# First block of a fused scan and expert kernel: the second product in plain fp32, and the weight remainders moved

## The chip, the cores and the metric

The kernel runs on one core of one Trainium2 chip. The core has TensorE (PE, matrix products, with its weight loads shown apart as PEld), VectorE (DVE), ScalarE (ACT), GpSimd (POOL) and SyncE (SP, which here only issues DMAs). The metric is the device time of one execution in microseconds. Three executions of the kernel before took 844.75, 845.05 and 848.32 us; their median is 845.05 us.

## What is computed

```python
# 1. a gated linear scan: q, k, v, alpha are [4, 8, 768, 48]
for t in range(S):
    state = alpha[:, :, t, :, None] * state + einsum('bhd,bhe->bhde', k[:, :, t], v[:, :, t])
    y[:, :, t] = einsum('bhd,bhde->bhe', q[:, :, t], state)
x = y.transpose(0, 2, 1, 3).reshape(3072, 384)
# 2. a dense layer: w_in [384, 2048], w_out [2048, 384]
h = x @ w_in
x = (h - np.tanh(h)) @ w_out
# 3. a top-1 mixture of 8 experts on these rows: argmax of x @ w_gate picks the expert,
#    out[mask] = gate_w * sigmoid(x @ w_output_gate) * (relu(x @ w1[e]) @ w2[e])
```

Everything is wanted in float32. The router takes an argmax of products, so part 2 has to be close to full float32 precision.

## The kernel before

**Tiling.** The 3072 tokens are eight blocks `j` of 384 (`TB`). In a block the dense layer runs over 16 slices `f` of 128 hidden features (`NF`). A slice is one `h_step` (the first product: three chunks of 128 input features, then tanh on ScalarE and h - tanh(h) on VectorE) and one `x_step` (the second product, for three groups of 128 tokens, added up over the 16 slices in three PSUM banks `x0` to `x2`). The scan is cut into units `u` of a block and a pair of heads, four units to a block; the units of block `j + 1` run between the dense slices of block `j`, one unit to four slices. The four slices `f % 4` of such a group are called phases 0 to 3 here: phase 0 has `score` and `update` of the unit, phase 2 its `readout`, phase 3 `turn_k`, the scan over its decays (`prep_q1`) and `scale_k`.

**Split products.** A product of two float32 matrices is made of three products in `F32R`: each operand is split into a rounded copy (`WH`, `gg[:, 0]`) and a remainder (`WL`, `gg[:, 1]`), and high x high, low x high and high x low are added up. So an `h_step` is nine matmuls of 384 columns (L401) and an `x_step` nine of 400 columns (L425). The 400 are 384 of `w_out` and 16 that stand for the two router matrices: `gate_turn` transposes a slice of `w_out` through PSUM (L369, copied by ScalarE at L371), and `gate` multiplies it by the router's weights (L377).

**Weights.** They arrive as 64-bit words that hold float64 values. `narrow` turns them into float32 on VectorE with three integer operations (L332, L334, L336), here on 768 columns at a time: 384 of `w_in` and 384 of `w_out`. `split_w` then writes the rounded copy on ScalarE (L361) and the remainder on GpSimd (L362). All of this is done in the first block, in `first_block`, for slices that lie one or two ahead of the products; two slices are prepared ahead of the block. From the second block on the weights only are read.

**Order.** In the first block the instructions of each engine stand in the order in which the program is written: `first_block(f)` writes the split of slice `f + 1`, the conversion of slice `f + 2`, the first product of slice `f`, then `head` (the `gate` of the slice and the unit's matmuls), h - tanh(h), `middle` (the second product of slice `f - 1` and the unit's vector work), and last `gate_turn(f + 1)`. From the second block on a scheduler sets the order. An engine takes its instructions strictly in order.

Of the kernel before, what the change touches and what calls it, by code (L numbers as in the profile page):

```python
# [63 lines left out]
def tile_kernel(ctx, tc, aps, outs):  # L64
# [12 lines left out]
    wp = wst_.enter_context(tc.tile_pool(name="wp", bufs=1))  # L77
    moe = ExitStack()
# [36 lines left out]
    WH = wp.tile([128, NF, DM + DG], F32R, name="WH")  # L115
    WL = wp.tile([128, NF, DM + DG], F32R, name="WL")
# [222 lines left out]
    def load_w(f):  # L339
        if wide:  # L340
            t = stg.tile([128, 2 * DM], I64, tag="wst", name="wst")
        else:
            t = stg3.tile([128, 2 * DM], F32, tag="w32", name="w32")
        wt[f] = t
        sp.dma_start(out=t, in_=aps["wio"][f].rearrange("p s c -> p (s c)"))

    px, gw, gated = {}, {}, {}

    def conv(f):
        w = wt.pop(f)  # L350
        if wide:
            t = stg3.tile([128, 2 * DM], I32, tag="w32", name="w32")
            yield from narrow(t, w)
            w = t.bitcast(F32)
        gw[f] = w
        if f + STG < NF:
            load_w(f + STG)

    def split_w(f):
        c = slice(0, 2 * DM)  # L360
        act.copy(WH[:, f, c], gw[f])  # L361
        pool.tensor_tensor(out=WL[:, f, c], in0=gw[f], in1=WH[:, f, c].bitcast(F32), op=ALU.subtract)  # L362


    def gate_turn(f):
        ps = psa.tile([128, 512], F32, tag="at", name="pso")
        w = gw.pop(f)
        for k in range(KC):
            pe.transpose(ps[:, k * 128:(k + 1) * 128], w[:, DM + k * 128:DM + (k + 1) * 128], ident)  # L369
# [4 lines left out]
    def gate(f):  # L374
# [20 lines left out]
    def h_begin(j, f, kcs):  # L395
        if kcs[0] == 0:
            begun[f] = psh.tile([128, 512], F32, tag="h", name="psh")
        for kc in kcs:
            c = slice(kc * 128, (kc + 1) * 128)
            for n, (w, x) in enumerate(((WH, 0), (WH, 1), (WL, 0))):  # L400
                pe.matmul(begun[f][:, 0:TB], w[:, f, c], xT[j][:, x, kc], start=(kc + n == 0), stop=(kc == KC - 1 and n == 2))  # L401

    def h_step(j, f, between=()):
# [4 lines left out]
        for step in between[:1]:  # L408
# [5 lines left out]
        for step in between[1:]:  # L414
            step()
# [3 lines left out]
    def x_step(j, f, gg):  # L419
        if f == 0:  # L420
            px[j] = [psx.tile([128, 512], F32, tag=f"x{a}", name=f"x{a}") for a in range(NA)]
        for a in range(NA):
            n = 0
# [279 lines left out]
    for u in range(NP):  # L703
        weave(chain(u))
        if u + 1 < NP:
# [10 lines left out]
            for f in list(gw):  # L716
                split_w(f)
# [474 lines left out]
```

## Time and profile before

| | |
|---|---|
| median of three executions | 845.05 us |
| the profiled execution | 845.42 us |
| its span | 843.6 us |
| PE busy, matmuls | 806.4 us (96%) |
| DVE busy | 478.1 us (57%) |
| ACT busy | 350.5 us (42%) |
| POOL busy | 164.0 us (19%) |
| mean granted TensorE clock | 0.974 of full |

The page also cuts the span into 40 slices of 21 us. Each digit below is a tenth: the busy share of an engine, or, in the row PEclk, the granted clock of TensorE. The first block of the dense layer lies in the slices 3 to 7.

```
PE   6788889999999999999999999999999999999995
DVE  6878886856756765765765654455443434434321
POOL 1023242011200110010020020012222414424321
PEclk 8798899999999999999999999999999999999998
```

Such a page is read from the stage outward: the totals say that PE is nearly always busy, but they are a mean over stages, and in the first slices PE has gaps, its clock is lower, and VectorE is as busy as PE.

### The profile page before, as it was taken

The numbers are of one execution on the slowest core, as the hardware profiler recorded it, in microseconds if no ns is written. First come the engines' busy times: TensorE is split into PE (matmuls) and PEld (weight loads), VectorE is DVE, ScalarE is ACT, GpSimd is POOL, SyncE is SP. The second block draws the span as 40 slices with busy tenths as digits, with TensorE's granted clock in tenths as the row PEclk, the third lists the DMA queues.
The fourth block names the chain that finished last, engine by engine and source line by source line (L and its number), as shares of the span: only waits on it lengthen the run. The fifth ranks groups of instructions, "written<-read, shape, count | busy, mean of one in ns | idle before, by whom it ended". The sixth has DMA issues, their size and how long they took to land.

```text
span 843.6 us, 17092 instructions
## 1 busy us (share of the span) xinstructions
PE 806.4 (96%) x6736; PEld 761.5 (90%) x6736; DVE 478.1 (57%) x1002; ACT 350.5 (42%) x783; POOL 164.0 (19%) x136
## 2 busy tenths in 40 slices
PE   6788889999999999999999999999999999999995
PEld 4577889999999999999999999999999999999995
DVE  6878886856756765765765654455443434434321
ACT  4544454533433433443433433335343434445431
POOL 1023242011200110010020020012222414424321
PEclk8798899999999999999999999999999999999998
DMA  9465442773322332242232220024335336325400
GB/s 272 144 223 184 144 125 57 236 244 100 102 83 64 83 103 64 68 124 65 65 103 82 64 76 19 15 99 135 133 136 202 115 105 217 103 102 206 155 26 30
DMA packets 64361, 98.55 MB, mean 117 GB/s; under 512 B 20236, under 2 KB 52769, under 8 KB 64273
## 3 DMA queue, kind: packets, MB, share of 16 engines
q1 hardware_dynamic: 60864, 87.91, 33.9%
q0 software_dynamic: 3408, 9.47, 3.0%
q8 instruction: 55, 0.90, 0.4%
q14 instruction: 34, 0.27, 0.1%
HBM read 72.13 MB, written 16.25 MB: 105 GB/s over the span
## 4 chain that ended last, share of the span: by engine, by line
PE 80%; DVE 6%; issue 5%; DMA 3%; ACT 2%; SPq 1%; POOL 1%; POOLq 0%; DVEq 0%; ACTq 0%
PE x L425 24%; PE psh L401 22%; PE o L950 11%; PE psf L922 10%; PE psy L302 4%; PE psy L238 3%; PE psu L264 2%; DVE w L334 2%; DMA raw<-raw 2%; PE pst L222 1%; PE pst L901 1%; ACT kt L200 1%; PE pso L377 1%; DMA s<-w 1%; DVE w L336 1%
## 5 line engine op out<-in xcount | busy, mean ns | idle before, releaser
L425 PE MATMUL x<-WH,gg 128*128 128x400 f32 x768 | 215.4, 356 | 1.0 <-DVE gg L416 0.7
L401 PE MATMUL psh<-xT,WH 128*128 128x384 f32 x768 | 204.2, 343 | 1.3 <-DMA xT<-y 1.2
L425 PEld LDWEIGHTS x<-WH,gg 128*128 128x128 f32 x768 | 140.5, 191 | 6.2 <-DVE gg L416 1.7
L401 PEld LDWEIGHTS psh<-xT,WH 128*128 128x128 f32 x768 | 138.4, 189 | 3.1 <-issue 1.6
L425 PE MATMUL x<-WL,gg 128*128 128x400 f32 x384 | 133.5, 349 | 0.0
L401 PE MATMUL psh<-xT,WL 128*128 128x384 f32 x384 | 130.1, 339 | 0.0
L411 DVE TENSOR_TENSOR t<-psh,t 128x384 f32<-128x384 f32 x128 | 70.9, 554 | 98.9 <-ACT t L407 98.2
L407 ACT ACTIVATE t<-psh 128x384 f32<-128x384 f32 x128 | 62.6, 489 | 130.1 <-PE psh L401 129.1
L950 PE MATMUL o<-hi,hh 128*128 128x384 f32 (+2 forms) x440 | 115.1, 338 | 0.0
L922 PE MATMUL psf<-xe,hi 128*128 128x256 f32 (+6 forms) x432 | 109.4, 338 | 0.0
L416 DVE TENSOR_TENSOR gg<-t,gg 128x384 fp32r<-128x384 f32 x128 | 73.7, 575 | 52.6 <-ACT gg L413 51.9
L413 ACT CAST gg<-t 128x384 fp32r<-128x384 f32 x128 | 65.5, 511 | 73.3 <-DVE t L411 72.3
L928 DVE SCALAR_TENSOR_TENSOR hh<-psf,hh 128x384 fp32r<-128x384 f32 (+3 forms) x96 | 40.9, 447 | 91.1 <-ACT hh L926 91.0
L950 PEld LDWEIGHTS o<-hi,hh 128*128 128x128 f32 (+2 forms) x440 | 78.3, 185 | 1.2 <-DVE hh L928 0.2
L922 PEld LDWEIGHTS psf<-xe,hi 128*128 128x128 f32 x432 | 75.8, 188 | 2.7 <-issue 0.3
L950 PE MATMUL o<-lo,hh 128*128 128x384 f32 (+1 forms) x232 | 77.7, 337 | 0.0
L926 ACT ACTIVATE hh<-psf 128x256 fp32r<-128x256 f32 (+6 forms) x72 | 34.8, 484 | 94.1 <-PE psf L922 78.6
L197 POOL TENSOR_TENSOR kt<-kh,rP 128x384 f32<-128x384 f32 x24 | 20.3, 845 | 273.0 <-PE psy L239 230.8
L425 PEld LDWEIGHTS x<-WL,gg 128*128 128x128 f32 x384 | 73.1, 190 | 0.1
L401 PEld LDWEIGHTS psh<-xT,WL 128*128 128x128 f32 x384 | 72.4, 189 | 0.6
L922 PE MATMUL psf<-xe,lo 128*128 128x256 f32 (+6 forms) x216 | 72.0, 333 | 0.0
L857 POOL TENSOR_TENSOR lo<-s,hi 128x768 fp32r<-128x768 f32 (+1 forms) x24 | 48.9, 2039 | 94.8 <-ACT hi L856 94.3
(141 smaller groups left out, 1130.0 us busy)
## 6 DMA issues: line engine op xcount, KB each, us to landing
raw<-raw SPq DMA_DIRECT2D x32, 579.5 KB, 4.5
wst<-wio SPq DMA_DIRECT2D x16, 768.0 KB, 4.4
s<-w SPq DMA_DIRECT2D x24, 512.0 KB, 3.8
s<-w SPq DMA_DIRECT2D x32, 384.0 KB, 5.3
xT<-y SPq DMA_DIRECT2D x96, 72.0 KB, 2.3
rows<-blank SPq DMA_DIRECT2D x8, 772.0 KB, 4.9
WV<-vw SPq DMA_DIRECT2D x32, 144.0 KB, 2.3
VZ<-vn SPq DMA_DIRECT2D x60, 72.0 KB, 2.4
```

Of the source, the lines that this page charges most:

```text
L302: pe.matmul(o, w, m, start=(c + x == 0), stop=(x == 1), skip_group_check=True)
L401: pe.matmul(begun[f][:, 0:TB], w[:, f, c], xT[j][:, x, kc], start=(kc + n == 0), stop=(kc == KC - 1 and n == 2))
L407: act.activation(out=t, in_=ps[:, 0:TB], func=AF.Tanh)
L411: dve.tensor_tensor(out=g, in0=ps[:, 0:TB], in1=t, op=ALU.subtract)
L413: act.copy(gg[:, 0], g)
L416: dve.tensor_tensor(out=gg[:, 1], in0=g, in1=gg[:, 0].bitcast(F32), op=ALU.subtract)
L425: pe.matmul(px[j][a][:, 0:DG], gg[:, gi, a * 128:(a + 1) * 128], w[:, f, DM:], start=(f == 0 and n == 0), stop=(f == NF - 1 and n == 2))
L857: (dve, pool)[i % 2].tensor_tensor(out=lo, in0=t, in1=hi.bitcast(F32), op=ALU.subtract)
L922: pe.matmul(ps[:, 0:n], w[:, kc, fs], xe[:, x, kc], start=(i == 0), stop=(i == 3 * KC - 1))
L926: act.activation(out=hh[:, 0:n], in_=ps[:, 0:n], func=AF.Relu)
L928: dve.scalar_tensor_tensor(out=hh[:, o:o + c.stop - c.start], in0=ps[:, c], scalar=0.0, in1=hh[:, c].bitcast(F32), op0=ALU.max, op1=ALU.su ...
L950: pe.matmul(po[q][m][0:p.stop - p.start, 0:DM], hh[:, p], w[:, f], start=(f == 0 and i == 0), stop=(f == NFE - 1 and i == len(parts) - 1))
```

## The change

In the first block the second product is one plain fp32 matmul of the unsplit `h - tanh(h)` with the unsplit weights `WR` (three instructions of 400 columns to a slice in place of nine; the profile shows a plain fp32 matmul as two). The split of the activations (L413, L416) falls away in this block. The weights have separate tiles now: `IH`, `IL` for `w_in`, `OH`, `OL` and the unsplit `WR` for `w_out`. `narrow` runs on 384 columns twice, in place of 768 once, and writes the half for `w_out` into `WR`. The remainders of `w_in` (`low_in`) are made on VectorE, not on GpSimd. Those of `w_out` (`low_out`) are made on VectorE too, but only two of them at the end of the first block and the other 14 in the second block, which is the first that reads them; their tiles take over the places of `WR`. GpSimd does no weight work any more. `scale_k` is written after `gate_turn(f + 1)` in phase 3, so that ScalarE copies `wT` first. The lines that choose between 64-bit and 32-bit weights, and the allocation of the tiles, are left out of the diff.

```diff
     def conv(f):
-        w = wt.pop(f)
         if wide:
-            t = stg3.tile([128, 2 * DM], I32, tag="w32", name="w32")
-            yield from narrow(t, w)
-            w = t.bitcast(F32)
-        gw[f] = w
+            t = stg3.tile([128, DM], I32, tag="w32", name="w32")
+            plain(f)
+            w = wt.pop(f)
+            yield from narrow(t, w[:, 0:DM])
+            gw[f] = t.bitcast(F32)
+            act.copy(IH[:, f], gw[f])
+            yield from narrow(WR[f][:, 0:DM].bitcast(I32), w[:, DM:])
...
-    def split_w(f):
-        c = slice(0, 2 * DM)
-        act.copy(WH[:, f, c], gw[f])
-        pool.tensor_tensor(out=WL[:, f, c], in0=gw[f], in1=WH[:, f, c].bitcast(F32), op=ALU.subtract)
+    def low_in(f):
+        dve.tensor_tensor(out=IL[:, f], in0=gw.pop(f), in1=IH[:, f].bitcast(F32), op=ALU.subtract)
+
+    def low_out(f):
+
+        OL[f] = wo.tile([128, DG], F32R, tag="w", name="OL")
+        dve.tensor_tensor(out=OL[f], in0=WR.pop(f), in1=OH[:, f].bitcast(F32), op=ALU.subtract)
...
-        c = slice(2 * DM, 2 * DM + 2 * E)
-        gl = ap2.tile([128, 2 * E], F32, tag="gl", name="gl")
-        act.copy(gl, pl)
-        act.copy(WH[:, f, c], pl)
-        gated[f] = gl, c
-
-    def gate_low(f):
-        gl, c = gated.pop(f)
-        dve.tensor_tensor(out=WL[:, f, c], in0=gl, in1=WH[:, f, c].bitcast(F32), op=ALU.subtract)
+        act.copy(WR[f][:, DM:DG], pl)
...
         g = t
         dve.tensor_tensor(out=g, in0=ps[:, 0:TB], in1=t, op=ALU.subtract)
+        if j == 0:
+            return g
         gg = g3.tile([128, 2, TB], F32R, tag="gg", name="gg")
         act.copy(gg[:, 0], g)
...
-            for gi, w in ((0, WH), (1, WH), (0, WL)):
-                pe.matmul(px[j][a][:, 0:DG], gg[:, gi, a * 128:(a + 1) * 128], w[:, f, DM:],
...
+            ts = slice(a * 128, (a + 1) * 128)
+            parts = ((gg[:, ts], WR[f]),) if j == 0 else ((gg[:, 0, ts], OH[:, f]), (gg[:, 1, ts], OH[:, f]), (gg[:, 0, ts], OL[f]))
+            for n, (g, w) in enumerate(parts):
+                pe.matmul(px[j][a][:, 0:DG], g, w, start=(f == 0 and n == 0), stop=(f == NF - 1 and n == len(parts) - 1))
...
             for f in list(gw):
-                split_w(f)
+                low_in(f)
...
-        if f + 1 < NF:
-            split_w(f + 1)
-        if nconv < NF:
-            weave(conv_next())
+        new = [conv_next()] if nconv < NF else []
...
             elif ph == 2:
                 readout(u)
+            act.copy(OH[:, f], WR[f])
+            if f + 1 < NF:
+                low_in(f + 1)
+            for g in new:
+                for _ in range(4 if wide else 0):
+                    next(g)
 
         def middle():
+            weave(*new)
...
                 x_step(*pend)
                 turn_k(u)
                 weave(prep_q1(u))
-                scale_k(u)
                 weave(prep_q2(u))
...
-        gg = h_step(0, f, (head, middle))
-        gate_low(f)
+        gg = h_step(0, f, (head,))
+        middle()
+        if f >= NF - 2:
+            low_out(f - NF + 2)
...
         if f + 1 < NF:
             gate_turn(f + 1)
-        else:
+        if ph == 3:
+            scale_k(u)
+        if f == NF - 1:
...
+            if j == 1 and f + 2 < NF:
+                low_out(f + 2)
             gg = h_step(j, f)
```

**VectorE, a slice of phase 3 in the first block, before.** `w` is the float32 word being built, `t` becomes h - tanh(h), `P`, `rP` and `X` are the decays of the unit.

```order
L332 TENSOR_SCALAR w_817<-wst 128x768
L334 SCALAR_TENSOR_TENSOR w_817<-wst,w_817 128x768
L336 SCALAR_TENSOR_TENSOR w_817<-wst,w_817 128x768
L411 TENSOR_TENSOR t<-psh,t 128x384
L184 SCALAR_TENSOR_TENSOR P<-raw,ones_116 128x391
L187 TENSOR_SCALAR rP<-P 128x6
L188 RECIPROCAL rP<-rP 128x6
L204 TENSOR_TENSOR X_120<-raw,P 128x384
```

The same place now:

```order
L374 TENSOR_TENSOR IL<-w_785,IH 128x384
L336 TENSOR_SCALAR w_831<-wst 128x384
L338 SCALAR_TENSOR_TENSOR w_831<-wst,w_831 128x384
L340 SCALAR_TENSOR_TENSOR w_831<-wst,w_831 128x384
L336 TENSOR_SCALAR WR<-wst 128x384
L419 TENSOR_TENSOR t<-psh,t 128x384
L338 SCALAR_TENSOR_TENSOR WR<-wst,WR 128x384
L340 SCALAR_TENSOR_TENSOR WR<-wst,WR 128x384
L188 SCALAR_TENSOR_TENSOR P<-raw,ones_119 128x391
L191 TENSOR_SCALAR rP<-P 128x6
L192 RECIPROCAL rP<-rP 128x6
L208 TENSOR_TENSOR X_124<-raw,P 128x384
```

The remainder `IL` stands ahead, the conversion is two chains of three short operations, and four of the six stand ahead of h - tanh(h), as all three did before.

**ScalarE, from phase 3 into phase 0, before.** `kt` are the six pieces of `scale_k`, `wT` is the transposed slice for the next `gate`.

```order
L381 CAST WH<-pso 128x16
L413 CAST gg<-t 128x384
L224 COPY ktok<-pst 128x384
L200 ACTIVATE kt<-kh,rP 128x64 x6
L371 COPY wT<-pso 128x384
L361 CAST WH<-w_817 128x768
L407 ACTIVATE t<-psh 128x384
```

The same place now:

```order
L780 CAST OH<-WR 128x400
L366 CAST IH<-w_831 128x384
L228 COPY ktok<-pst 128x384
L387 COPY wT<-pso 128x384
L204 ACTIVATE kt<-kh,rP 128x64 x6
L415 ACTIVATE t<-psh 128x384
L394 COPY WR<-pso 128x16
```

`wT` has moved ahead of the six pieces of `kt`, and the 768-column rounding of the next slice's weights has become two copies (`OH`, `IH`) further ahead.

**VectorE, where the first block ends and the second begins, before** (from the last slice's split of the activations on; `r` and `lz` are the rows handed to the router).

```order
L416 TENSOR_TENSOR gg<-t,gg 128x384
L386 TENSOR_TENSOR WL<-gl,WH 128x16
L176 TENSOR_TENSOR kh<-raw,Ex 128x384
L184 SCALAR_TENSOR_TENSOR P<-raw,ones_116 128x391
L187 TENSOR_SCALAR rP<-P 128x6
L204 TENSOR_TENSOR X_120<-raw,P 128x384
L188 RECIPROCAL rP<-rP 128x6
L411 TENSOR_TENSOR t<-psh,t 128x384
```

The same place now, from the decays of the last slice's unit to h - tanh(h) of the second block's first slice:

```order
L192 RECIPROCAL rP<-rP 128x6
L208 TENSOR_TENSOR X_123<-raw,P 128x384
L379 TENSOR_TENSOR OL<-WR,OH 128x400 x3
L180 TENSOR_TENSOR kh<-raw,Ex 128x384
L379 TENSOR_TENSOR OL<-WR,OH 128x400
L188 SCALAR_TENSOR_TENSOR P<-raw,ones_119 128x391
L379 TENSOR_TENSOR OL<-WR,OH 128x400
L191 TENSOR_SCALAR rP<-P 128x6
L208 TENSOR_TENSOR X_124<-raw,P 128x384
L419 TENSOR_TENSOR t<-psh,t 128x384
```

The five remainders `OL` in this piece stand between the decays of the coming units. One stands ahead of the piece, and ten follow, the last of them ahead of h - tanh(h) of the second block's fifth slice. From the middle of the second block on, the rows of every engine are the same as before but for names and numbers.

## Rows read from the trace of the kernel before

**Rows 1.** ScalarE's timeline, first block: start us, us, engine, line, operation, tiles; slices 0, 4, 8, 12, 15

```profile
46.06 0.49 ACT L407 ACTIVATE t<-psh 128x384 f32<-128x384 f32 x1 [2.17 <-PE psh L401]
...
71.16 0.48 ACT L407 ACTIVATE t<-psh 128x384 f32<-128x384 f32 x1
...
97.09 0.48 ACT L407 ACTIVATE t<-psh 128x384 f32<-128x384 f32 x1
...
123.76 0.48 ACT L407 ACTIVATE t<-psh 128x384 f32<-128x384 f32 x1
...
142.05 0.49 ACT L407 ACTIVATE t<-psh 128x384 f32<-128x384 f32 x1 [1.03 <-PE psh L401]
```

**Rows 2.** Busy us of PE, PEld, DVE, ACT, POOL, then clock, in two stretches

```profile
71.00:97.00 26.00, 22.77 (x197) 21.80 (x197) 21.83 (x35) 13.26 (x38) 8.13 (x4) 0.89 0.52 168
147.00:200.00 53.00, 52.84 (x527) 49.54 (x527) 36.24 (x88) 23.87 (x58) 6.46 (x10) 1.00 0.67 210
```

**Rows 3.** Timelines of VectorE and GpSimd, slice 7 (phase 3)

```profile
88.67 0.55 DVE L332 TENSOR_SCALAR w<-wst 128x768 int32<-128x768 int32 x1
89.26 2.48 DVE L334 SCALAR_TENSOR_TENSOR w<-wst,w 128x768 int32<-128x768 int32 x1
91.78 0.96 DVE L336 SCALAR_TENSOR_TENSOR w<-wst,w 128x768 int32<-128x768 int32 x1
...
88.80 2.12 POOL L362 TENSOR_TENSOR WL<-w,WH 128x768 fp32r<-128x768 f32 x1 [4.01 <-DVE y L311]
```

**Rows 4.** TensorE's timeline and the chain of waits (start us, us), slice 8 (phase 0)

```profile
96.50 1.46 PE L377 MATMUL pso<-wg,wT 128*128 128x16 f32 x6 [3.23 <-ACT wT L371]
...
99.44 1.16 PE psu L264 x12
100.60 3.02 PE x L425 x9
```

**Rows 5.** TensorE's timeline, slice 14 (phase 2)

```profile
134.41 0.49 PE L369 MATMUL pso<-cst,w 128*128 128x128 f32 x3
134.66 0.60 PE L401 MATMUL psh<-xT,WH 128*128 128x384 f32 x2
...
136.33 0.73 PE L377 MATMUL pso<-wg,wT 128*128 128x16 f32 x6
137.00 0.47 PE L302 MATMUL psy<-X,SS 48*64 48x64 f32 x8
...
138.22 0.63 PE L425 MATMUL x<-WH,gg 128*128 128x400 f32 x2
...
139.96 0.49 PE L369 MATMUL pso<-cst,w 128*128 128x128 f32 x3
```

**Rows 6.** TensorE's timeline, slice 0 (score, update)

```profile
46.52 0.27 PE L238 MATMUL psy<-X,kt 48*64 48x64 f32 x1
...
47.37 0.72 PE L264 MATMUL psu<-VZ,ktok 128*64 128x96 f32 x12
```

**Rows 7.** Lines L238, L264, L222 and L401 alone: count: ns min/median/max

```profile
L238 PE MATMUL psy<-X,kt x336: 218/218/366, 46.5 to 526.0; 48*64 48x64 f32 x168
...
L264 PE MATMUL psu<-VZ,ktok x360: 246/246/421, 9.3 to 526.7; 128*64 128x96 f32 x180
...
L222 PE MATMUL pst<-cst,kh x96: 270/272/475, 7.3 to 521.2; 128*128 128x128 f32 x96
...
L401 PEld LDWEIGHTS psh<-xT,WH x768: 186/188/333, 39.5 to 587.7; 128*128 128x128 f32 x192
```

**Rows 8.** Timelines ahead of the first block: VectorE, ScalarE, TensorE

```profile
29.48 0.55 DVE L244 TENSOR_TENSOR X<-pss,cst 128x384 f32<-128x384 f32 x1
...
29.82 0.83 ACT L361 CAST WH<-w 128x768 fp32r<-128x768 f32 x1
...
45.26 0.58 PE L401 MATMUL psh<-xT,WH 128*128 128x384 f32 x2 [1.22 <-DMA xT<-y]
```

**Rows 9.** Line L416 alone, VectorE, 384 columns, two inputs

```profile
L416 DVE TENSOR_TENSOR gg<-t,gg x128: 528/559/2182, 49.0 to 590.2; 128x384 fp32r<-128x384 f32 x128
```

More of the change, by code (lines that the diff above doesn't have):

```diff
@@ L112, in tile_kernel @@
     ones1 = ap1.tile([128, AW], F32, name="ones1")
-    WH = wp.tile([128, NF, DM + DG], F32R, name="WH")
-    WL = wp.tile([128, NF, DM + DG], F32R, name="WL")
+    IH = wp.tile([128, NF, DM], F32R, name="IH")
+    IL = wp.tile([128, NF, DM], F32R, name="IL")
+    OH = wp.tile([128, NF, DG], F32R, name="OH")
+    OL, WR = {}, {}
     X0 = [ap1.tile([128, TB], F32, name=f"X0{i}") for i in range(2)]
@@ L340, in load_w, with plain @@
         if wide:
[L341 to L345 removed]
+            wt[f] = t = stg.tile([128, 2 * DM], I64, tag="wst", name="wst")
+            sp.dma_start(out=t, in_=aps["wio"][f].rearrange("p s c -> p (s c)"))
+        else:
+            gw[f] = stg3.tile([128, DM], F32, tag="w32", name="w32")
+            plain(f)
+            sp.dma_start(out=gw[f], in_=aps["wio"][f, :, 0])
+            sp.dma_start(out=WR[f][:, 0:DM], in_=aps["wio"][f, :, 1])
     px, gw, gated = {}, {}, {}
+    def plain(f):
+        WR[f] = (ap1 if f == NF - 1 else wo).tile([128, DG], F32, tag="w", name="WR")
     def conv(f):
[L350 removed]
         if wide:
[L352 to L355 removed]
+            t = stg3.tile([128, DM], I32, tag="w32", name="w32")
+            plain(f)
+            w = wt.pop(f)
[3 more added lines that the diff above has]
+            yield from narrow(WR[f][:, 0:DM].bitcast(I32), w[:, DM:])
+        else:
+            act.copy(IH[:, f], gw[f])
         if f + STG < NF:
             load_w(f + STG)
[L359 to L362 removed]
+    def low_in(f):
[3 more added lines that the diff above has]
+        dve.tensor_tensor(out=OL[f], in0=WR.pop(f), in1=OH[:, f].bitcast(F32), op=ALU.subtract)
     def gate_turn(f):
         ps = psa.tile([128, 512], F32, tag="at", name="pso")
[L367 removed]
         for k in range(KC):
[L369 removed]
+            pe.transpose(ps[:, k * 128:(k + 1) * 128], WR[f][:, k * 128:(k + 1) * 128], ident)
         wT = g3.tile([128, KC, 128], F32, tag="gg", name="wT")
@@ L399, in h_begin @@
             c = slice(kc * 128, (kc + 1) * 128)
-            for n, (w, x) in enumerate(((WH, 0), (WH, 1), (WL, 0))):
+            for n, (w, x) in enumerate(((IH, 0), (IH, 1), (IL, 0))):
                 pe.matmul(begun[f][:, 0:TB], w[:, f, c], xT[j][:, x, kc], start=(kc + n == 0), stop=(kc == KC - 1 and n == 2))
@@ L407, in h_step @@
         act.activation(out=t, in_=ps[:, 0:TB], func=AF.Tanh)
-        for step in between[:1]:
+        for step in between:
             step()
@@ L422, in x_step @@
         for a in range(NA):
-            n = 0
-            for gi, w in ((0, WH), (1, WH), (0, WL)):
-                pe.matmul(px[j][a][:, 0:DG], gg[:, gi, a * 128:(a + 1) * 128], w[:, f, DM:],
-                          start=(f == 0 and n == 0), stop=(f == NF - 1 and n == 2))
-                n += 1
+            ts = slice(a * 128, (a + 1) * 128)
+            parts = ((gg[:, ts], WR[f]),) if j == 0 else ((gg[:, 0, ts], OH[:, f]), (gg[:, 1, ts], OH[:, f]), (gg[:, 0, ts], OL[f]))
+            for n, (g, w) in enumerate(parts):
+                pe.matmul(px[j][a][:, 0:DG], g, w, start=(f == 0 and n == 0), stop=(f == NF - 1 and n == len(parts) - 1))
     def scores(pool_, r, n):
@@ L681, in narrowed @@
         for g in half:
-            for _ in range(3 if wide else 0):
+            for _ in range(6 if wide else 0):
                 next(g)
```

3 lines of the change are left out of this document (1 added, 2 removed).

## Prediction

> **What bounds the kernel now.** I read the page's parts 1 and 2 first, then windows by stage, then ScalarE's timeline for the start of each tanh, then the chain of waits, and last the timelines of PE, DVE and POOL around the places that the chain names. From the second block on PE bounds: in the stretch from 147 to 200 us it is busy 52.84 of 53.00 us at a granted clock of 1.00 [rows 2]. In the first block it does not. There PE is busy 22.77 of 26.00 us at a clock of 0.89, and DVE 21.83 [rows 2]. The tanh of slices 0, 4, 8, 12 and 15 start at 46.06, 71.16, 97.09, 123.76 and 142.05 us [rows 1], so four slices take 25.10, 25.93 and 26.67 us, the last three 18.29. That is the stretch in which the change works.
>
> Three things make a group of four slices that long, and the reader should see each. *First*, DVE is held up by POOL. In slice 7 the operation L334 takes 2.48 us where its twin L336 of the same 768 columns takes 0.96, and POOL's remainder L362 runs from 88.80 for 2.12 us just then [rows 3]. The difference is 1.52 us, and the chain of waits shows it in two or three slices of every four. *Second*, the late DVE makes the decays late, ScalarE does the six pieces of kt ahead of wT, and PE waits 3.23 us for wT at the head of phase 0 [rows 4]. *Third*, after this wait PE runs at half its clock, 1.2 GHz: the gate takes 1.46 us (0.67 in slice 14), an update 1.16 us, the second product 3.02 us (1.74) [rows 4, 5].
>
> **The change part by part.** *The second product on PE.* Removed are nine matmuls, 138.22 to 139.96, so 1.74 us a slice at full clock [rows 5]; that is nine times 0.18 and some 0.1 at the head. Added are three plain fp32 matmuls, each two instructions in the profile. No fp32 row is as wide as 400 columns, so I bound it. From above: fp32 instructions of 64, 96 and 128 columns take 218, 246 and 270 ns [rows 7], about 0.82 ns for each further column, which is two TensorE cycles at 2.4 GHz; 400 columns then stream for 0.33 us, and with the 0.01 us that the split matmuls have on top of their columns an instruction is 0.34 us. From below: twelve updates of 96 columns are issued in 0.72 - 0.25 = 0.47 us [rows 6], 0.043 us each, which would be one cycle a column (0.18 us at 400) if their two column halves ran one after the other. Score starts its two halves in pairs, so I take the halves as concurrent and 0.34, an estimate: 6 x 0.34 + 0.1 = 2.14 us a slice, 0.40 more than now. On PE alone the change is a loss.
>
> *The cover on DVE.* One group of four now has 21.83 us of DVE work [rows 2]. The remainder of the activations leaves and that of w_in comes, both 384 columns with two inputs (0.56 us, [rows 9]): nothing. Six operations on 384 columns replace three on 768: by half of 0.55 and 0.96 plus some 0.08 to fill and 0.03 to wait for each that follows its own result, 2 x (0.35 + 0.58 + 0.52) = 2.9 us against 2.5, so 4 x 0.4 = 1.6 us more (0 to 2.5). The holds by POOL go, two in that window: -3.0 us (0 if POOL is not what holds DVE). Sum 20.4 us.
>
> *A group of four on PE, after.* From slice 14 [rows 5]: four turns of 0.25, first products of 1.67, gates of 0.67, and one readout of 1.22; from slice 0, at full clock, a score of 0.85 and an update of 0.55 [rows 6]; one turn_k like a gate turn, 0.25; four second products of 2.14. That is 1.00 + 6.68 + 2.68 + 1.22 + 0.85 + 0.55 + 0.25 + 8.56 = 21.8 us. DVE's 20.4 us lie beside it, so PE is the bound, by little. ScalarE now copies wT ahead of kt, so the gate no longer waits; the six kt (some 1.5 us) and the copies behind them can still be late for score and update, and I give 0.9 us for that. A group of 22.7 us.
>
> *The sum up to slice 15.* Slices 0 to 4 have one second product fewer (none pends in slice 0): 20.6 against 25.1, less 4.5. Slices 4 to 12: 45.4 against 52.6, less 7.2. Slices 12 to 15 lack a phase 3 (0.25 + 1.67 + 0.67 + 2.14 + 0.25 = 5.0): 17.7 against 18.3, less 0.6. Together 12.3 us less.
>
> *What is paid outside.* The second products of slices 14 and 15 come after that point: +0.8. Ahead of the block DVE gets a remainder and the longer conversions: L244 at 29.48 must now stand behind the remainder of slice 0, which waits for ScalarE's rounding, begun at 29.82 [rows 8] and, on half of the 768 columns that take 0.83 us now, some 0.5 us long; with both conversions the last unit of the prologue is 1.9 us later. PE waits there for a DMA until 45.26, 1.22 us [rows 8], which covers most: +0.6 (0 to 1.9). In the second block 14 remainders of 400 columns, about 0.48 us each between issues, are 6.7 us of DVE work. DVE was busy 36.24 of 53 us there [rows 2], so there is room, but the order puts them into the first five slices, between operations on which PE waits: I take 0.5 us, from 0 to all 6.7. POOL and SP get no new work, and ScalarE (13.26 of 26 us, [rows 2]) trades a rounding of 768 columns and one of the activations for copies of 384 and 400: nothing.
>
> Sum: -12.3 + 0.8 + 0.6 + 0.5 = -10.4 us. The profiled execution took 845.42 us (a span of 843.6 and 1.8 around it), so 835.0; it lies 0.37 above the median, so **834.7 us**. After the middle of the second block the rows are those of before, and PE bounds: the gain should neither grow nor shrink there.
>
> **The rivals.** *Weight loads come into the open.* Now they hide: a load of 128 columns shows 186 ns [rows 7], yet a split matmul and its load follow the last in 0.18 us. The gate's six instructions, of 16 columns each, take 0.67 us [rows 5], so a bare load is 0.11 us at most. If fp32 loads did not run ahead, 6 x 0.1 x 17 slices would give back 10.2 us: 845. The Trainium skill, TensorE: Matmul & The Clock Gate, section Part 3, The mechanism, says that a weight load overlaps running matmuls only where its row group differs, which is never so here. By that rule the sum would be this 845; the trace speaks against it for split matmuls, which use all rows and hide their loads [rows 5, 7], and no run here shows it for wide fp32.
>
> *PE stays at half clock at the heads of groups.* If DVE or ScalarE is still late there by the 3 us of now, gate, update and second product cost 0.8 + 0.6 + 1.6 us more, and part of the wait stays: some 3.5 us a group, three groups, 845. Against it stands wT ahead of kt.
>
> *The remainders delay the second block* by their whole 6.7 us: 841. For it speaks their place in the queue, against it the two slices of products that PE has in hand.
>
> *fp32 streams a column a cycle.* Then a second product takes 1.2 us, DVE's 20.4 us and a wait of 0.9 bound a group at 21.3, 1.4 less, 5.3 over the 3.75 groups, and slices 14 and 15 save 1.9: 834.7 - 5.3 - 1.9 = 827.5.
>
> *Slower: fp32 costs more than its columns show*, so that each 400-column instruction takes 0.67 us (four cycles a column, or half clock throughout). Then every slice has 2.0 us more, 17 times: 869. It decides from 0.34 + 10.4 / (6 x 17) = 0.44 us an instruction, where the change is worth nothing; at 0.48 it is slower by 0.5%. That the change doesn't do what it says I rule out: the order shows three plain matmuls where nine stood.
>
> **How the numbers follow.** Forecast (830 to 840) 0.57; open loads or half clock, 845, 0.17 together; remainders, 841, 0.10; a cycle a column, 827, 0.09; slower, 869, 0.07. The range from 827 to 843 holds the first, the third, the fourth and a part of the second. A measurement here tells about 0.5% from no change, 4.2 us. Faster by more (below 840.8): 0.57 + 0.09 + half of the remainders and a little of the second, 0.72. Slower (above 849.3): 0.07. The rest, 0.21, lies within.
>
> **What would show it.** In the profile after: plain fp32 matmuls of 400 columns about 0.34 us apart with no load between; DVE's 384-column integer operations near 0.56 us without one of 2 us; no PE wait over 1 us for wT, and a clock near 1.00 from slice 4 on; tanh starts of slices 4, 8, 12 some 22.7 us apart; slice 15 near 130 us. It is wrong if an fp32 instruction is far from 0.34 us, if DVE is still held with POOL idle, or if PE waits for DVE in the second block.

## The result and the profile after

The kernel after takes 832.42 us (median of four executions, 831.33 to 833.43) against 845.44 us of the kernel before beside it (four executions): a ratio of 0.9839, 95% interval 0.9813 to 0.9866. The profiled execution took 833.43 us, with a span of 831.6; that of before 845.42 and 843.6. So 12.0 us of span went. By the medians it is 13.0 us.

ScalarE's timeline, the start of tanh in slices 0, 4, 8, 12 and 15, to be set against [rows 1]:

```profile
47.27 0.49 ACT L415 ACTIVATE t<-psh 128x384 f32<-128x384 f32 x1 [1.86 <-PE psh L409]
...
68.20 0.47 ACT L415 ACTIVATE t<-psh 128x384 f32<-128x384 f32 x1
...
90.23 0.47 ACT L415 ACTIVATE t<-psh 128x384 f32<-128x384 f32 x1
...
112.25 0.48 ACT L415 ACTIVATE t<-psh 128x384 f32<-128x384 f32 x1
...
129.04 0.49 ACT L415 ACTIVATE t<-psh 128x384 f32<-128x384 f32 x1 [1.11 <-PE psh L409]
```

Four slices now take 20.93, 22.03 and 22.02 us, the last three 16.79. From slice 0 to slice 15 it is 81.77 us in place of 95.99: 14.2 us less. Windows over one group of the first block and over the head of the second (busy PE, PEld, DVE, ACT, POOL, then clock), as [rows 2]:

```profile
65.00:87.00 22.00, 21.67 (x184) 17.59 (x183) 19.42 (x42) 11.57 (x33) 0.00 (x0) 1.00 0.59 196
130.00:183.00 53.00, 51.92 (x488) 46.63 (x487) 40.38 (x99) 21.87 (x55) 7.18 (x10) 1.00 0.65 207
```

PE is busy 21.67 of 22.00 us at a clock of 1.00, its upper level of 2.4 GHz, where it was busy 22.77 of 26.00 at 0.89; DVE has 19.42 us of work and POOL none. PE bounds the first block. At the head of the second block PE now has gaps that it did not have: 1.1 us of 53 are idle, where 0.2 were.

The line of the second product alone (count: ns min/median/max), then PE's timeline from slice 7 into 8, and one of the weight loads (PEld). A line of a timeline is a run of like instructions with the start of the first:

```profile
L434 PEld LDWEIGHTS x<-WR,t x96: 186/190/192, 52.9 to 136.0; 128*128 128x128 f32 x96
L434 PE MATMUL x<-WR,t x96: 498/499/603, 52.9 to 136.3; 128*128 128x400 f32 x96
```

```profile
85.41 2.26 PE L434 MATMUL x<-WR,t 128*128 128x400 f32 x6
87.50 0.49 PE L226 MATMUL pst<-cst,kh 128*128 128x128 f32 x3
...
89.75 0.74 PE L393 MATMUL pso<-wg,wT 128*128 128x16 f32 x6
91.66 0.72 PE L268 MATMUL psu<-VZ,ktok 128*64 128x96 f32 x12 [0.33 <-ACT psu L259]
```

```profile
86.16 0.19 PEld L434 LDWEIGHTS x<-WR,t 128*128 128x128 f32 x1
```

A plain second product holds PE for 87.50 - 85.41 = 2.09 us, 0.35 an instruction. In the trace the first of the six takes 0.42 us, and the others start 0.336 us apart. The weight loads lie inside that: the one at 86.16 starts together with the matmul ahead of it and has ended 0.14 us before its own matmul starts at 86.50. So 0.34 us is the time of the columns, and not 0.17 us of columns with a load of 0.19 us behind them, which would come to nearly the same sum. The gate takes its short time and waits for nothing ([rows 4]: 1.46 after a wait of 3.23). VectorE in slice 7, against [rows 3]: no operation of 2.48 us is left, the two-input operations of 384 columns take 0.56.

```profile
83.18 0.35 DVE L336 TENSOR_SCALAR w<-wst 128x384 int32<-128x384 int32 x1
83.57 0.56 DVE L338 SCALAR_TENSOR_TENSOR w<-wst,w 128x384 int32<-128x384 int32 x1
84.16 0.56 DVE L340 SCALAR_TENSOR_TENSOR w<-wst,w 128x384 int32<-128x384 int32 x1
```

**Where 12.0 us went.** The first tanh comes 1.21 us later (47.27 against 46.06), slices 0 to 15 take 14.22 us less, and the stretch from slice 15 to slice 4 of the third block (tanh at 228.77 before and 217.80 after) takes 2.04 more: 88.76 against 86.72 us. Windows over exactly that stretch, before and then after:

```profile
142.05:228.77 86.72, 86.56 (x836) 81.73 (x835) 59.16 (x147) 37.86 (x93) 10.54 (x14) 1.00 0.53 161
```

```profile
129.04:217.80 88.76, 87.68 (x830) 80.47 (x829) 65.13 (x160) 37.24 (x93) 10.22 (x14) 1.00 0.51 155
```

PE has 1.12 us more work there and 0.92 us more idle time. Of the work, the two plain products of slices 14 and 15 are at most 2 x (2.09 - 1.74) = 0.7 us; where the rest comes from was not looked into. The waits of PE in it (total us, times, longest) name VectorE, which has 6.0 us more to do, the remainders of `w_out`:

```profile
PE x L434 <- DVE gg L424: 0.5, 1, 0.5
PE x L434 <- DVE lz L471: 0.4, 1, 0.4
```

From there to the end the kernel after is another 1.03 us shorter; on that see the last section.

### The profile page after: what moved, and what is told of

Its sections match the earlier page's. It is cut to its first block, busy times and chain, and to the rows that moved or that the text cites. A ratio compares the mean times of both kernels' runs of the same rounds, so it can differ in the third digit from the quotient of the medians.

```text
span 831.6 us, 16944 instructions
## 1 busy us (share of the span) xinstructions
PE 803.4 (97%) x6688; PEld 745.6 (90%) x6688; DVE 476.7 (57%) x1050; ACT 343.6 (41%) x767; POOL 131.5 (16%) x120
## 4 chain that ended last, share of the span: by engine, by line
PE 84%; issue 5%; DVE 4%; ACT 3%; DMA 2%; SPq 1%; POOL 1%; POOLq 0%; ACTq 0%; DVEq 0%
PE x L434 26%; PE psh L409 23%; PE o L964 11%; PE psf L936 11%; PE psy L306 4%; PE psu L268 2%; PE psy L242 2%; PE pst L226 1%; PE warm L685 1%; PE pst L915 1%; ACT kt L204 1%; DMA raw<-raw 1%; PE pso L393 1%; DMA s<-w 1%; POOL out L982 1%
## 5 line engine op out<-in xcount | busy, mean ns | idle before, releaser
L409 PE MATMUL psh<-xT,IH 128*128 128x384 f32 x768 | 204.0, 342 | 0.0
L434 PE MATMUL x<-OH,gg 128*128 128x400 f32 x672 | 186.0, 351 | 1.1 <-DVE gg L424 0.5
L409 PEld LDWEIGHTS psh<-xT,IH 128*128 128x128 f32 x768 | 138.3, 189 | 1.0
L409 PE MATMUL psh<-xT,IL 128*128 128x384 f32 x384 | 129.9, 338 | 0.0
L434 PEld LDWEIGHTS x<-OH,gg 128*128 128x128 f32 x672 | 121.5, 188 | 5.4 <-DVE gg L424 1.1
L434 PE MATMUL x<-OL,gg 128*128 128x400 f32 x336 | 115.9, 345 | 0.0
L424 DVE TENSOR_TENSOR gg<-t,gg 128x384 fp32r<-128x384 f32 x112 | 63.6, 568 | 50.1 <-ACT gg L423 47.7
L423 ACT CAST gg<-t 128x384 fp32r<-128x384 f32 x112 | 57.3, 512 | 57.3 <-DVE t L419 56.1
L409 PEld LDWEIGHTS psh<-xT,IL 128*128 128x128 f32 x384 | 72.4, 188 | 0.8
L434 PEld LDWEIGHTS x<-OL,gg 128*128 128x128 f32 x336 | 63.2, 188 | 0.0
```

Source lines behind the costliest of these rows:

```text
L424: dve.tensor_tensor(out=gg[:, 1], in0=g, in1=gg[:, 0].bitcast(F32), op=ALU.subtract)
L434: pe.matmul(px[j][a][:, 0:DG], g, w, start=(f == 0 and n == 0), stop=(f == NF - 1 and n == len(parts) - 1))
```

## Experiments

Twelve kernels ran. The first columns are the median of four to ten executions and its ratio, with the 95% interval, to executions of before that ran beside that kernel (their medians were 845.44 to 845.69 us). The others are read from ScalarE's timeline in the one profiled execution: the first tanh, the time from tanh to tanh of slices 0-4, 4-8, 8-12 and 12-15, and their sum. Gains "up to slice 15" below are differences of these sums.

| kernel | us | ratio | first | 0-4 | 4-8 | 8-12 | 12-15 | sum |
|---|---|---|---|---|---|---|---|---|
| before | 845.4 | | 46.06 | 25.10 | 25.93 | 26.67 | 18.29 | 95.99 |
| b_order | 844.42 | 0.9982 (0.9968-0.9995) | 45.88 | 24.73 | 25.14 | 26.28 | 17.05 | 93.20 |
| b_dve | 840.29 | 0.9933 (0.9909-0.9956) | 46.17 | 23.51 | 25.28 | 24.26 | 17.27 | 90.32 |
| b_both | 838.58 | 0.9922 (0.9893-0.9951) | 46.72 | 22.61 | 23.91 | 23.90 | 17.28 | 87.70 |
| after | 832.42 | 0.9839 (0.9813-0.9866) | 47.27 | 20.93 | 22.03 | 22.02 | 16.79 | 81.77 |
| a_load | 847.07 | 1.0012 (0.9997-1.0027) | 46.16 | 23.89 | 25.84 | 25.81 | 18.21 | 93.75 |
| a_pool | 834.65 | 0.9877 (0.9862-0.9892) | 46.56 | 21.46 | 22.52 | 22.52 | 16.75 | 83.25 |
| a_kt | 837.06 | 0.9892 (0.9866-0.9918) | 47.21 | 21.02 | 22.78 | 22.76 | 19.17 | 85.73 |
| a_hyb | 839.64 | 0.9933 (0.9917-0.9949) | 46.30 | 24.05 | 23.53 | 23.54 | 19.49 | 90.61 |
| a_norest | 834.67 | 0.9865 (0.9841-0.9888) | 46.82 | 20.92 | 22.01 | 22.02 | 16.78 | 81.73 |
| a_four | 833.77 | 0.9859 (0.9836-0.9883) | 46.78 | 20.93 | 22.01 | 22.00 | 16.80 | 81.74 |
| a_pro | 831.87 | 0.9853 (0.9820-0.9887) | 45.08 | 20.93 | 22.00 | 22.01 | 16.80 | 81.74 |
| a_procar | 831.33 | 0.9832 (0.9813-0.9851) | 45.71 | 20.92 | 21.61 | 21.62 | 16.41 | 80.56 |
| a_best | 842.73 | 0.9954 (0.9936-0.9972) | 46.14 | 28.10 | 22.98 | 22.98 | 17.63 | 91.69 |

The runs set the prediction's theory against three rivals: the order of `wT` and `kt` alone made the gain; POOL never held VectorE; the plain product is itself a loss.

### The change taken apart from the side of before

**b_order** moves `kt` behind `wT` and nothing else.

```diff
                 weave(prep_q1(u))
-                scale_k(u)
                 weave(prep_q2(u))
...
             gate_turn(f + 1)
-        else:
+        if ph == 3:
+            scale_k(u)
+        if f == NF - 1:
```

> The kernel before, with one change alone: the six pieces of kt are written after the transposes of the next slice, so that ScalarE copies wT ahead of them; POOL keeps the remainders and the second product stays split. Theory (the late VectorE is what the first block waits for, the order on ScalarE only decides who waits): wT comes some 1.5 us earlier, but score and update then wait for kt, whose decays are as late as before; part of PE's 3.2 us of waiting and its half clock at the heads of groups stay. A group of four shrinks by at most 1 us of 25.9; 841 to 845 us. Rival (the order is the main cause, the half clock that follows the wait for wT included): the wait for wT falls under 1 us, the gate after it takes 0.67 us and not 1.46, groups of 23 us or less, 834 to 836 us.

**b_dve** makes the 768-column remainder on VectorE, behind the conversion.

```diff
         if f + 1 < NF:
-            split_w(f + 1)
+            split_w(f + 1, False)
         if nconv < NF:
             weave(conv_next())
+        if f + 1 < NF:
+            split_low(f + 1, dve)
```

> The kernel before, with one change alone: in the first block the remainder of the weights (768 columns) is made on VectorE behind the conversion, not on POOL. If POOL's remainder is what holds VectorE, no two-input VectorE operation of 768 columns takes over 1.1 us any more (2.48 in slice 7 before) and none of 384 over 0.6; the holds of 1.5 us, two or three to a group, go, and four remainders of about 1.0 us come: VectorE 21.8 - 3.0 + 4.0 = 22.8 us a group, so the time stays within 3 us of before, 842 to 848. Rival (the long operations wait for data, not for POOL): they stay at 2 us and more, VectorE has 26 us a group, 855 us or more. Second rival (the POOL holds are the whole loss): 838 us or less.

**b_both** has the two edits.

> Both edits of the two other kernels at once: the remainder of the weights on VectorE and wT ahead of kt, the second product still split. It is the change without its plain fp32 product and without moving the remainders of w_out into the second block. Theory (VectorE's work bounds the first block, and the plain product is what takes it off VectorE): a group is bound by VectorE's 22.8 us of work and waits of about 1 us, 23.8 us against 25.9, 3.75 groups, so 837 to 840 us: some 60% of the gain, the rest being the plain product's. Rival (POOL and the order explain everything): PE bounds with 21.8 - 1.6 = 20.2 us of products a group, 21.5 with waits, 828 to 831 us, and the plain product is a loss. Second rival (VectorE's order delays the decays all the same): 844 us or more.

b_order gains 2.8 us up to slice 15, of which 1.3 are left in the median, and its waits show what the theory said: PE's wait is shared between `wT` and the copy into `psu` behind the late `kt` (waits of PE, 90 to 97.3 us):

```profile
PE psu L264 <- ACT psu L255: 1.7, 1, 1.7
PE pso L377 <- ACT wT L371: 1.3, 1, 1.3
```

It is not a clean test of the order alone: VectorE meets POOL's remainder in three slices of the group 4 to 8 there, at 70.89, 82.10 and 88.28 us, where in before it met it in two, and has 23.26 us of work in place of 21.79.

b_dve gains 5.7 us up to slice 15 and 5.4 in the median, more than the 3 us that were expected at most. The operation that took up to 2.5 us now takes 0.96 each time:

```profile
L334 DVE SCALAR_TENSOR_TENSOR w<-wst,w x16: 958/959/961, 27.0 to 123.8; 128x768 int32<-128x768 int32 x16
```

So the long ones were POOL's doing. VectorE's work in slices 4 to 8 is 22.2 us (the theory had 22.8), hardly more than the 21.8 of before although it makes four remainders of 0.95 us itself. So VectorE's work in a group did not fall at all, and yet the block became shorter. What differs is the place: both holds of that group in before, 1.5 us each, stand in slices 6 and 7, ahead of the decays; b_dve has 0.95 us in each of the four slices. PE's wait for `wT` in slices 4 to 8 fell from 3.2 us to 1.9:

```profile
PE pso L382 <- ACT wT L376: 1.9, 1, 1.9
```

b_both gains 8.3 us, close to the sum of the two, and stands at 838.58, inside the 837 to 840 of the theory: 58% of the gain up to slice 15. Its slices 4 to 8 still show VectorE at 22.16 of 23.91 us, a PE wait of 1.7 us for `psu`, and a clock of 0.93:

```profile
69.33:93.24 23.91, 22.19 (x195) 21.25 (x195) 22.16 (x38) 13.25 (x39) 0.00 (x0) 0.93 0.54 170
```

The remaining 5.9 us come with the rest of the change: the plain product, the remainders that it lets go, the conversion and the rounding in two halves and their new places. No run takes these apart fully; a_hyb below takes back the plain product in a quarter of the slices.

### POOL beside VectorE, from the side of after

**a_load** puts a POOL operation into the kernel after that nobody waits for.

```diff
                 low_in(f + 1)
+            if f >= 2:
+                pool.tensor_tensor(out=load, in0=IH[:, f - 2:f]..., in1=IL[:, f - 2:f]..., op=ALU.subtract)
```

> The kernel after, with a subtraction of 768 columns on POOL in each of the slices 2 to 15 of the first block, of numbers long made, into a tile that nobody reads: nobody waits for it, so whatever it does to others is contention. Theory (POOL's two-input operations hold VectorE's): VectorE operations with two inputs from SBUF that start beside it grow by about 1.5 us, operations that read PSUM do not, VectorE has 19.4 + 4 x 1.5 = 25.4 us a group, PE waits, and the time rises by some 3 us a group over 3.5 groups: 840 to 846 us. Rival (POOL never held VectorE, the long operations of before came from waiting on data): every VectorE operation keeps its 0.35 or 0.56 us and the time stays at 832, within 1 us.

VectorE's and POOL's timelines in slice 7:

```profile
88.24 0.35 DVE L337 TENSOR_SCALAR w<-wst 128x384 int32<-128x384 int32 x1
88.63 2.07 DVE L339 SCALAR_TENSOR_TENSOR w<-wst,w 128x384 int32<-128x384 int32 x1
90.74 0.56 DVE L341 SCALAR_TENSOR_TENSOR w<-wst,w 128x384 int32<-128x384 int32 x1
```

```profile
88.47 1.82 POOL L785 TENSOR_TENSOR load<-IH,IL 128x768 f32<-128x768 f32 x1 [3.88 <-DVE IL L375]
```

The operation that starts while POOL runs takes 2.07 us in place of 0.56 and ends 0.41 us after POOL does; its twin behind it takes 0.56. By the Trainium skill, SBUF — State Buffer, section Who interferes with whom, VectorE and GpSimd share one pair of ports under an exclusive lock, and a VectorE instruction with two SBUF inputs contends with a GpSimd instruction that reads SBUF; the trace agrees. Slices 4 to 8:

```profile
70.05:95.89 25.84, 23.86 (x186) 18.92 (x187) 25.32 (x42) 11.86 (x35) 7.30 (x5) 0.93 0.52 169
```

VectorE's work is 25.32 us (25.4 was expected) of 25.84, and the clock is 0.93. Up to slice 15 the load costs 12.0 us, and the kernel is no faster than before (a ratio of 1.0012). It came out 1 us above the expected range. This is the clearest run of the set: nobody waits for the operation, so contention alone costs here nearly as much as the change had gained. It is not a share of that gain, for the load stands on top of VectorE's own remainders; what taking POOL out of before is worth is b_dve's figure.

**a_pool** undoes the part of the change that moved the remainders of `w_in`, now of 384 columns.

```diff
-        dve.tensor_tensor(out=IL[:, f], in0=gw.pop(f), ...)
+        (dve if f < 2 else pool).tensor_tensor(out=IL[:, f], in0=gw.pop(f), ...)
```

> The kernel after, with the remainders of w_in on POOL again from slice 2 on, now 384 columns; nothing else. Theory (a VectorE operation that meets a POOL remainder is held until that ends): the remainder takes about 0.9 us on POOL and holds the one long VectorE operation that it meets by some 0.8 us, while VectorE no longer makes it (0.55 us): 19.45 + 4 x 0.25 = 20.5 us a group, still under PE's 21.7, so groups of four stay at 22.0 to 22.3 us and the time within 1.5 us of the kernel after. Rival (any remainder on POOL brings back the waits of before): 24 us a group or more, 839 us or more.

Groups of 22.52 us and 834.65: a little past the theory's 22.3 and its 1.5 us. VectorE's work is 19.6 us, under PE's; what costs is which operation is held. VectorE's timeline in slice 7 (phase 3), with POOL's remainder from 86.59 to 87.80:

```profile
86.59 1.21 POOL L374 TENSOR_TENSOR IL<-w,IH 128x384 fp32r<-128x384 f32 x1 [3.49 <-ACT IH L366]
```

```profile
86.86 1.77 DVE L188 TENSOR_TENSOR_SCAN P<-raw,ones 128x391 f32<-128x391 f32 x1
```

The scan of the decays takes 1.77 us in place of 0.97, and everything for the next phase 0 hangs on it: `rP`, `kt`, and the copy into `psu`, for which PE now waits 0.8 us in place of 0.33.

### The order on ScalarE, from the side of after

**a_kt** writes `scale_k` ahead of `gate_turn` again (the reverse of the diff of b_order).

> The kernel after, with the six pieces of kt ahead of wT on ScalarE again, as before. Theory (with VectorE early, the order on ScalarE matters little): the decays are ready by the time ScalarE has copied ktok, so wT moves by the 1.45 us of the six pieces and ends some 0.7 us after PE has finished the first product; PE waits 0.3 to 0.8 us a group for it, no half clock follows, 833 to 836 us. Rival (the order was the main cause): the wait of 3 us and the half clock come back, 25 us a group, 840 us or more.

Measured 837.06, between the two. In two of the groups it is the theory: PE waits 0.55 us for `wT`, 22.8 us a group. In the last group the clock falls (TensorE's timeline, slice 12, and a window inside its second product):

```profile
113.92 0.84 PE L393 MATMUL pso<-wg,wT 128*128 128x16 f32 x6 [0.55 <-ACT wT L387]
...
115.88 0.72 PE L268 MATMUL psu<-VZ,ktok 128*64 128x96 f32 x12 [0.28 <-ACT psu L259]
116.53 3.97 PE L434 MATMUL x<-WR,t 128*128 128x400 f32 x6
```

```profile
117.50:119.50 2.00, 2.00 (x5) 1.01 (x4) 1.93 (x6) 0.00 (x0) 0.00 (x0) 0.50 0.30 74
```

The second product behind the two waits takes 3.97 us in place of 2.3, and the granted clock inside it is 0.50, the level of 1.2 GHz. Slices 12 to 15 take 19.17 us in place of 16.79. The same waits in slices 4 and 8 had no such effect, so that the waits bring on the half clock is not shown. In this execution the order is worth 1.6 us by itself, and 2.4 more with the spell at half clock in the last group.

### The second product split again in four slices

**a_hyb** keeps everything of the change but splits the product in slices 2, 6, 10 and 14. VectorE has two more operations in such a slice, the remainder of the activations and that of `w_out`, which falls away in the second block. The lines for the tiles are left out.

```diff
-        if j == 0:
+        if j == 0 and f not in SPLIT:
             return g
...
+        if f in SPLIT:
+            low_out(f)
```

> The kernel after, but in four slices of the first block (2, 6, 10, 14) the second product is split again: activations and w_out get their remainders there, nine matmuls in place of three plain ones. Theory (PE bounds the block after the change, with 2.5 us a group to spare on VectorE, and a plain product costs PE 0.47 us more than a split one): VectorE gets 1.0 us a group, 20.5 us, PE loses 0.47 us a group, so groups of 21.5 to 21.7 us against 22.0 and 1.5 to 2 us less in all. Rival (the spare time of VectorE lies in the wrong places): groups of 22.0 or more, nothing gained or 1 us lost.

The theory missed: 839.64 us, groups of 23.53. VectorE's work is 20.4 us as expected. PE's busy time did not fall (21.84 us against 21.70 in after). But VectorE stands still in the middle of the split slice (VectorE's and ScalarE's timelines, slice 6):

```profile
84.79 0.56 DVE L426 TENSOR_TENSOR gg<-t,gg 128x384 fp32r<-128x384 f32 x1 [1.42 <-ACT gg L425]
```

```profile
83.41 0.53 ACT L782 CAST OH<-WR 128x400 fp32r<-128x400 f32 x1
83.83 0.51 ACT L368 CAST IH<-w 128x384 fp32r<-128x384 f32 x1
84.25 0.51 ACT L425 CAST gg<-t 128x384 fp32r<-128x384 f32 x1
```

The remainder of the activations needs ScalarE's rounded copy, which stands there behind two other copies; VectorE waits 1.42 us for it, with the conversion and the decays of slice 7 queued behind. PE's waits in slices 4 to 8 are for what comes behind, the decays `X` and the copy into `psu`:

```profile
PE psu L270 <- ACT psu L261: 0.9, 1, 0.9
PE psy L244 <- DVE X L210: 0.8, 1, 0.8
```

So a plain product takes more off VectorE than the operations of 0.56 and 0.57 us: also this trip to ScalarE and back. PE's own 0.47 us were not to be had. What a_hyb lost up to slice 15 (8.8 us) is nearly all that it lost. Its first group, 24.05 us at a clock of 0.93, and its last slices, 19.49 us at 0.82, have spells at the lower clock besides, so not all of the loss is the trip.

### The remainders of w_out in the second block

**a_norest** leaves the 14 remainders out; **a_four** makes four in the first block, not two.

```diff
...
-(gg[:, 0, ts], OL[f]))
+(gg[:, 0, ts], OL[f] if f < 2 else OH[:, f]))
...
-            if j == 1 and f + 2 < NF:
-                low_out(f + 2)
```

> The kernel after, without the 14 remainders of w_out in the second block: VectorE does not make them, and the third part of the second product reads the rounded weights in their place from slice 2 on in every later block, so PE has the same matmuls and the rows are not those of the reference. Theory (the remainders pay little: VectorE has room there): 0.5 to 1.5 us less than the kernel after, 831 to 832, all of it ahead of the second block's sixth slice. Rival (they delay the second block by their whole 6.7 us, hidden in the result by a larger gain in the first): 826 us.

```diff
-        if f >= NF - 2:
-            low_out(f - NF + 2)
+        if f >= NF - 4:
+            low_out(f - NF + 4)
...
-            if j == 1 and f + 2 < NF:
-                low_out(f + 2)
+            if j == 1 and f + 4 < NF:
+                low_out(f + 4)
```

> The kernel after, with four remainders of w_out made in the first block, at its last four slices, in place of two at its last two, and 12 in the second block in place of 14. Theory (PE bounds the first block with over 2 us a group to spare on VectorE, while VectorE is what PE waits for at the head of the second block): slices 12 to 15 keep their times within 0.3 us, the head of the second block loses less, 0.3 to 1 us less in all, 831.4 to 832.1 us. Rival (VectorE has no room in slices 12 and 13): slice 15's tanh comes 0.5 us later and nothing is gained.

Both missed. a_norest is slower than after by 1.8 us in the stretch from slice 15 on (90.60 against 88.76). With the remainders gone the scheduler put VectorE's other work into another order, and PE waits for h - tanh(h):

```profile
PE psh L409 <- DVE t L419: 2.7, 2, 1.4
```

So the run tells nothing of the remainders alone. a_four keeps the first block as it was and takes 88.96 us for that stretch: nothing gained. Nor is the 0.9 us of idle time that after has more than before there all due to the remainders: b_order and b_dve, which have none in that stretch, idle there for 0.84 and 0.60 us, b_both for 0.25, where before idles for 0.16. What the remainders cost stays open, between nothing and about 1 us; that they do not cost their whole 6.7 us of VectorE's time is shown by after itself, whose stretch is 2.04 us longer.

### The prologue, and a better version

**a_pro** writes the weight work of slices 0 and 1 later; **a_procar** besides puts `carry(u)` ahead of `decay(u)`; **a_best** adds the four split slices. The diff is that of a_pro.

```diff
-            for _ in range(6 if wide else 0):
+            for _ in range(3 if wide else 0):
...
-            weave(*half)
-            for f in list(gw):
-                low_in(f)
...
-    half = [conv_next()]
-    narrowed(half)
+    weave(*half)
...
     K(NP)
+    low_in(0)
     fill(4)
-    weave(*half)
...
     weave(prep_q(NP))
+    weave(conv_next())
```

> The kernel after, with the weight work ahead of the first block written later: the w_out half of slice 0's conversion after the last readout of the prologue, slice 0's remainder after the scan that follows, and slice 1's conversion after the unit's decays, where VectorE was idle for 4.4 us. Theory (the prologue is 1.2 us longer than before because VectorE's longer conversions stand ahead of the two y that feed the last DMAs of the first xT): the last y starts 1.5 to 2 us earlier, the first tanh at 45.5 to 46.1 us (47.27 after, 46.06 before), and the whole kernel gains what the first tanh gains, 830.6 to 831.3 us. Rival (the DMA queue sets the first tanh): the first tanh stays at 47, 832.4.

> The kernel with the weight work written later in the prologue, and besides the copy of the carried state into psu ahead of the decay on ScalarE in phase 0. Theory (PE's last regular wait of 0.33 us a group is for that copy, 0.9 us late behind the decay): the wait goes, groups of 21.7 us against 22.0, 1 us less over the block than without it: a span of 828.4 to 829.0 us (829.4 without it, 831.6 after), a median of 830.5 to 831.3. Rival (the scan that needs the decay is then late in turn): groups stay at 22.0.

> All three edits: the prologue's weight work written later, the copy into psu ahead of the decay, and four slices with a split second product. If each gives what it should, the first tanh at 45.1 us, groups of 21.3 us, and a span 2.2 + 1.0 + 1.8 = 5 us under that of the kernel after: 826.6, a median near 828.5. If the split slices gain nothing, as the kernel without them: 830.5 to 831.3.

a_pro brings the first tanh to 45.08 us, 2.2 earlier, and its profiled span is 829.4, 2.2 under that of after. That is the theory, and a little more, but it is one execution. The median, 831.87 us, lies above the expected 830.6 to 831.3, and its ratio, 0.9853, is not below that of after, 0.9839, so a gain is not shown. The first tanh scatters as much: kernels with the prologue of after have it between 46.16 and 47.27, those with that of before between 45.88 and 46.72, and the three with the new one between 45.08 and 46.14. In a_procar PE is busy without a gap (window over slices 4 to 8, 21.61 of 21.61 us):

```profile
66.63:88.24 21.61, 21.61 (x185) 17.60 (x185) 19.44 (x42) 11.66 (x34) 0.00 (x0) 1.00 0.62 194
```

The 1.2 us that this saves up to slice 15 against a_pro are lost again, 0.6 in the prologue and 0.7 behind the block (89.52 us for the stretch from slice 15 on). At 831.33 us it can't be told from the kernel after. a_best missed both of its forecasts, at 842.73 us. Its groups 4 to 12 are 1.4 us each longer than those of a_procar, which the split slices explain; the first group, 28.10 us, is the larger part. Just ahead of it PE waits 3.4 us for a DMA, and then the granted clock is 0.50 up to slice 1:

```profile
PE psh L411 <- DMA xT<-y: 3.4, 1, 3.4
```

```profile
46.14:54.67 8.53, 7.50 (x55) 7.05 (x56) 4.54 (x9) 2.26 (x6) 0.00 (x0) 0.50 0.85 309
```

Why that DMA came late was not looked into.

## Why the prediction was right

The prediction was 834.7 us; 832.42 came. By its own steps:

- **The second product.** 2.14 us forecast, 2.09 measured. With it fall the rivals that rest on its price: open weight loads, a column a cycle, 0.67 us an instruction. These rivals count 17 second products, but the block has 16 (96 instructions), so their 845 and 869 us should be some 844 and 867; nothing hangs on it. The sentence that the prediction takes from the Trainium skill, TensorE: Matmul & The Clock Gate, section Part 3, The mechanism, does not hold by itself for these loads, which use all rows and lie inside instructions 0.336 us apart; the same section also has a case that the prediction leaves out, loads into the background weight buffer, which are pulled ahead.
- **VectorE.** 20.4 us a group forecast, 19.42 measured. Forgotten was that the remainder of the 16 router columns (L386, 0.17 us, one to a slice) goes too: 0.7 us. That POOL held VectorE is shown by b_dve and a_load. That the sum of VectorE's work is what bounds the block is only half right: b_dve became faster with as much work as before, with less of it in the two slices ahead of the decays.
- **PE.** 21.8 us of work forecast, 21.67 measured. The mis-sized term is the wait for ScalarE behind it, 0.9 us, measured 0.33. That is why the groups are 22.0 and not 22.7 us, and slices 0 to 15 give 14.2 us and not 12.3, although slices 0 to 4 took 20.93 us where 20.6 stood.
- **No wait for wT, full clock.** Right, and a_kt shows that it hangs on the order: half a microsecond of waiting came back, and once the half clock.
- **Outside.** The prologue cost 1.21 us in the profiled execution where 0.6 stood (0 to 1.9). PE's work behind slice 15 grew by 1.1 where 0.8 stood for the products of slices 14 and 15, which explain 0.7 of it. The head of the second block had 0.9 more idle time where 0.5 stood for the remainders, not all of it theirs. PE does wait for VectorE there, 0.5 and 0.4 us, which the prediction had named as a sign of being wrong; it stays small beside the 6.7 us of that rival. These took 1.3 us more than forecast, and 1.0 us that was not forecast came back later, though the prediction said that the gain would not grow there. The forecast of 10.4 became 12.0.
- **Profile and median.** The profiled execution of after lies 1.0 us above its median, where the prediction took the 0.37 of before. That is the other 0.6 of the 2.3 us between 834.7 and 832.42. That the forecast came so near is in part luck: the errors in these terms have both signs.

One step was right in its sum but too short in its reason: the prediction let the remainder of `w_in` take the place of that of the activations "for nothing". a_hyb shows that the two are not alike: the one waits on VectorE's queue for a copy that ScalarE has just been given, the other for one made earlier.

## What to carry to other kernels

Where an engine is late, look in its own timeline for operations that take a multiple of their twins, and see what another engine runs at that moment: work moved to an idle GpSimd can cost VectorE more than doing it there. Adding up an engine's work is not enough: look, too, at how much of it stands ahead of what others wait for. A precise but slower matrix product can pay, as it did here, when it takes a round trip over two other engines out of an in-order queue, as long as the stage is bound by those and not by PE. Count such a trade again once PE is the bound; in a_procar the last 0.3 us a group could be had and were lost again next door.

## What was not expected of the hardware

- POOL holds more than operations with two inputs from SBUF. In a_pool a one-input operation that starts in the middle of the POOL remainder of 82.10 to 83.10 is held (0.70 us in place of 0.35), while one that reads PSUM just ahead of it is not. The same pair shows in the other groups:

```profile
82.10 1.00 POOL L374 TENSOR_TENSOR IL<-w,IH 128x384 fp32r<-128x384 f32 x1 [4.54 <-ACT IH L366]
```

```profile
82.16 0.55 DVE L315 TENSOR_TENSOR y<-psy,y 128x384 fp32r<-128x384 f32 x1
82.62 0.70 DVE L336 TENSOR_SCALAR w<-wst 128x384 int32<-128x384 int32 x1
```

- A plain fp32 product of 400 columns takes two instructions, 2 x 0.336 = 0.67 us at 2.4 GHz, 4.0 cycles a column. The Trainium skill, FP8 and Floating Point Precision, section TensorE Precision Notes, gives true fp32 four passes; the trace agrees.
- From slice 15 of the third block (tanh at 274.12 and 263.03 us) to the end, where both kernels have the same instructions, before takes 569.48 us and after 568.57. The three kernels built on before show 569.4 to 569.6, the seven built on after that split no product in the first block 568.4 to 568.8. The difference lies in the dense blocks: from slice 15 of one block to slice 15 of the next it is 65.50 us in before and the three built on it, and 65.3 in all that are built on after. Up to the last tanh PE is busy without a gap at a clock of 1.00 in both. The weights lie in other tiles there; whether that is the cause was not tested.
